# Closing multiplies and second norms on GpSimd, early second queries and a later column of ones, in two transformer layers on one core

## The chip, the cores and the metric

One Trainium2 chip, one of its cores. A core has TensorE (matmuls; PE in the profile, PEld for its weight loads), VectorE (DVE), ScalarE (ACT), GpSimd (POOL), SyncE (SP, which here only issues DMAs), an on-chip memory (SBUF) and an accumulator memory for matmuls (PSUM). The metric is the time of one execution in microseconds; less is better.

## What is computed

Two equal layers. Each is attention with a residual, then a token mixer with a residual. The input is 2048 tokens x 640; 32 heads of width 20; the hidden width of the mixer is 1536. Weights are the same in both layers.

```python
def _A_ref(x, wqkv, wo):                       # attention
    qkv = (x @ wqkv) ... q, k, v = qkv[0], qkv[1], qkv[2]
    scores = jnp.einsum("bhqd,bhkd->bhqk", q, k) * (Dh ** -0.5)
    o = jnp.einsum("bhqk,bhkd->bhqd", _softmax(scores), v)
    return o ... @ wo
def _B_ref(x, w1, b1, w2, b2):                 # mixer over tokens
    u = _gelu(jnp.einsum("bsd,sf->bdf", _layernorm(x), w1) + b1)
    return (jnp.einsum("bdf,fs->bds", u, w2) + b2) transposed
x = x + _A_ref(_layernorm(x), A_wqkv, A_wo)
x = x + _B_ref(_layernorm(x), B_w1, B_b1, B_w2, B_b2)      # and both once more
```

The mixer norms x before `_B_ref` and again inside it; the kernel does both norms in one pass, and this is what the text calls the second norm (`ln_proc` with `twice`).

## The kernel before, in words

**Work.** The scores of one head group (4 heads), one block of 512 queries and one tile of 128 keys are a *unit* of four *cells*, each 128 x 512. A layer has 4 x 8 x 16 = 512 units, 2048 cells. TensorE writes scores into tiles S of three or two cells in turn (`emit_S`, `s_matmul`, L703). ScalarE turns a tile into exponentials P (`emit_exp`, L773). Some cells go to VectorE instead (`ve_admit`, L547): their scores lie in the bank Dt, and VectorE and GpSimd work out 2^x by a polynomial, two cells (a pair) at a time: ew (L563), shift to ey (L661, on GpSimd, or on VectorE by L589), square (L593), et (L597), result Pd. For Pd, GpSimd may first write a half (L644, `ve_base`) to which VectorE adds (L614); otherwise VectorE forms it in one longer step (L616). TensorE multiplies P and Pd by the values with a column of ones (Vaug) into acc (L1326, `emit_PV`), so acc holds the products and the sum of the exponentials.

**Closing a run.** The 16 units of a head group and query block are a *run*. When a run closes, `finish_run` (L791) makes VectorE transpose acc (L810), add an earlier part of the run if there is one (L818), take reciprocals (L823), multiply (`scaled`, L826) and transpose into attnT (L834). The out-projection (L1117, in the last query block L1155 and L960) adds the residual. `ln_proc` (L880) then norms x: statistics (L886, L889), aggregate (L893), variance (L898 for the second norm, L901), the power -1/2 on GpSimd (L903), and the apply (L907) on VectorE. After that come the products with w1 (L1068), which `end_tiles` (L950) ends together with the last out-projection.

**Order.** All engines run in an order that the program works out while it is built. It keeps a clock for each engine (`pem`, `dvm`, `acm`, `port`) with a planned duration of each step. VectorE's work is a list of `Proc`s, each with a rank and steps; `pump` takes the ready one with the lowest rank. A step with a fourth element true is *locked*: it does not start before the planned end of GpSimd's job (`port["pool"]`). When a step of at least 0.45 us that isn't locked starts, `ve_shift` may give GpSimd one job beside it (a shift, or else a base); `after_vector` makes that job wait for the VectorE instruction before it. How many cells VectorE takes follows from its planned backlog. TensorE fills the time between scores with queued work (`add_fill`: projections, out-projection, mixer products), by priority, and with matmuls on zeros (L762) where little is queued.

**Feeds.** `TokenFeed` starts layer 0: loads and norms tokens, transposes them (L1225), projects keys and queries (L1177) and values (L1201). At its start ScalarE clears the pad columns of Vaug, and VectorE sets the column of ones (`zero_values`, L1546). `MixFeed` starts layer 1 from the mixer of layer 0 (L1753 to L1775, then `y_fill`, L1685). While tokens arrive, attention already runs on the first four head groups of query blocks 0 and 1 (`early_qbs`), as far as keys and queries are there. The queries of block 1 are queued in `t_fill` (L1249) with the priority `base[tb] + 16.0 + 8.0 * g - 4`; a lower number goes first.

**The ends of a layer.** After the last exponential the rest of the queue is emptied with three PSUM banks (`tail_alloc`, L1458), then `end_tiles` adds the last head group's out-projection and norms the last two token tiles.

Of the kernel before, what the change touches and what calls it, by code (L numbers as in the profile page):

```python
# [25 lines left out]
DH = 20  # L26
# [39 lines left out]
VE_SPARE = 6  # L66
VE_ADD = (1.22, 1.03, 0.69)
POOL_DMA = 0.9

HOLD = 3  # L70
WARM_WAVES = 14
# [10 lines left out]
def kernel(  # L82
# [141 lines left out]
    def attention(st, x_in_ap, x_mid, uacc_l, feed, feed_stack):  # L224
# [40 lines left out]
        acm = dict(t=feed.act_free, over=0.0, next=0.06, procs=[])  # L265
        port = dict(pool=0.0, t=0.0)
        pieces = deque()
        acc_free = [0.0]
        kready, vready = {}, {}
        work = deque()  # L270
# [389 lines left out]
        def shift(engine, out_ap, in_ap):  # L660
            return engine.tensor_scalar(out=out_ap, in0=in_ap, scalar1=MANT_K / FIX, scalar2=-MANT_K * MANT_S,  # L661
                                        op0=ALU.mult, op1=ALU.add)

        def ve_shift(at, self_cost):
# [126 lines left out]
        def finish_run(run):  # L791
# [24 lines left out]
            def added(end):  # L816
                dst = box["T1"] if whole else part_view((qb, g))
                nc.vector.tensor_tensor(out=cols(dst), in0=cols(box["T1"]), in1=cols(part_view((qb, g))), op=ALU.add)  # L818

            def recip(end):  # L820
                box["v"] = box["T1"].rearrange("p (c i) -> p c i", i=32)
                box["r"] = ntmp.tile([128, 16], F32, name="rden")
                nc.vector.reciprocal(out=box["r"][:, 0:nb], in_=box["v"][:, :, DH])  # L823

            def scaled(end):
                nc.vector.tensor_tensor(out=T2[:, 0:nb, 0:DH], in0=box["v"][:, :, 0:DH],  # L826
                                        in1=box["r"][:, 0:nb].unsqueeze(2).to_broadcast([128, nb, DH]), op=ALU.mult)

            def back(end):
                if c0 == 0:  # L830
# [21 lines left out]
            def turned(end):  # L852
                if rest:
                    p = Proc(norm_rank(run), rest, end + DVE_NEXT, after=after if whole else None,
                             allow=lambda me: not whole or (bool(late) and (len(me.steps) > 1 or at_live[0] < NG + 4)))
                    p.norm = True
                    submit(p)
            first.after = turned
            first.allow = lambda me: not any(p in dvm["procs"] for p in ahead)
# [20 lines left out]
        def ln_proc(src, twice, get_dst, rank, ready, after, allow_apply=None, on_act=False, cheap=0.0):  # L880
# [14 lines left out]
            def veps(e):  # L895
                v = stat.tile([128, 1], F32, name="veps")
                if twice:
                    nc.vector.tensor_scalar(out=v[:], in0=box["mv"][:, 1:2], scalar1=1.0 + LN_EPS,  # L898
                                            scalar2=LN_EPS * LN_EPS, op0=ALU.mult, op1=ALU.add)
                else:  # L900
                    nc.vector.tensor_scalar_add(out=v[:], in0=box["mv"][:, 1:2], scalar1=LN_EPS)  # L901
                box["r"] = stat.tile([128, 1], F32, name="rstd")
                nc.gpsimd.tensor_tensor(out=box["r"][:], in0=v[:], in1=mhalf[:], op=ALU.pow)  # L903
                port["t"] = max(port["t"], e + POOL_NEXT) + 0.55

            def apply(e):
                nc.vector.tensor_scalar(out=get_dst(), in0=src, scalar1=box["mv"][:, 0:1],  # L907
                                        scalar2=box["r"][:, 0:1], op0=ALU.subtract, op1=ALU.mult)

            def shift(e):  # L910
                box["n"] = stat.tile([128, 1], F32, name="nmr")
# [15 lines left out]
            submit(Proc(rank, steps, ready, after=last,  # L927
                        allow=allow_apply and (lambda me: len(me.steps) > 1 or on_act or allow_apply())))

        def do_ln2(tt, x1s, end):  # L930
            def dst():
# [285 lines left out]
        def t_fill(tt, h_bf, ready, done):  # L1217
# [235 lines left out]
        for t in sums:  # L1453
            zero_wave(t[:, 0:512], True, True)
            zero_wave(t[:, 512:D], True, True, HALF / 2, D - 512)
        tail_banks = [sums[0][:, 1024:1536], None, None]

        def tail_alloc():  # L1458
            bank = tail_banks.pop()
            return bank if bank is not None else Dbank.alloc() if len(tail_banks) == 1 else misc.alloc()  # L1460
# [10 lines left out]
    class TokenFeed:  # L1471
        groups = 4
        early_qbs = (0, 1)
        ve_early = True
        act_helps = True
        act_free = 0.0
        warm_until = 5.6
# [28 lines left out]
        def begin(self, cx):  # L1506
# [36 lines left out]
            def zero_values(e):  # L1543
                nc.scalar.memzero(Vv[:, :, :, DH:VW])
                nc.scalar.memzero(Vv[:, :, 4 * self.groups, 0:32 - VW])
                cx.submit(cx.Proc(2.6, [(0.49, lambda e: nc.vector.memset(Vv[:, :, :, DH:DH + 1], 1.0), 0.0)], e + 5.0))  # L1546
# [46 lines left out]
    class MixFeed:  # L1593
        groups = 4
        early_qbs = (0, 1)
        ve_early = False
        act_helps = True
        act_free = 0.0
        warm_until = 0.0
# [283 lines left out]
```

## Time and profile before

| | |
|---|---|
| median of 3 runs | 1754.15 us (1754.06 to 1754.17) |
| the profiled execution | 1754.05 us |
| its span | 1752.3 us |
| TensorE busy | 1677.7 us (96%) |
| ScalarE busy | 1665.0 us (95%) |
| VectorE busy | 1534.9 us (88%) |
| GpSimd busy | 592.0 us (34%) |
| granted TensorE clock | full, in every slice |
| chain of work that ended last | ScalarE 50%, TensorE 25%, issue 22% |

Busy time is the time in which an engine worked on an instruction; instructions of one engine overlap a little, so single durations add up to more. A row of the groups names line, engine, operation, result and inputs, count, busy time, mean of one in ns, and the engine's idle time just before with what ended it. A row of the stretches names from and to, length, and for each engine busy time and instructions, then granted clock, DMA share and GB/s. A row of the timeline names start, duration, engine, line and what it is, and in brackets the idle time before it.

### The profile page before, as it was taken

The numbers are of one execution on the slowest core, as the hardware profiler recorded it, in microseconds if no ns is written. First come the engines' busy times: TensorE is split into PE (matmuls) and PEld (weight loads), VectorE is DVE, ScalarE is ACT, GpSimd is POOL, SyncE is SP. The second block draws the span as 40 slices with busy tenths as digits, with TensorE's granted clock in tenths as the row PEclk, the third lists the DMA queues.
The fourth block names the chain that finished last, engine by engine and source line by source line (L and its number), as shares of the span: only waits on it lengthen the run. The fifth ranks groups of instructions, "written<-read, shape, count | busy, mean of one in ns | idle before, by whom it ended". The sixth has DMA issues, their size and how long they took to land.

```text
span 1752.3 us, 43289 instructions
## 1 busy us (share of the span) xinstructions
PE 1677.7 (96%) x17891; PEld 663.4 (38%) x17891; DVE 1534.9 (88%) x2491; ACT 1665.0 (95%) x1498; POOL 592.0 (34%) x936
## 2 busy tenths in 40 slices
PE   8999999999999999999999999999999999999999
PEld 3333333333333344444434433233333333444455
DVE  7789999999999999998543469999999999999973
ACT  8999999999999999999779999999999999999970
POOL 2243443353544343332000023434434443434310
PEclk9999999999999999999999999999999999999999
DMA  4020000000122010133322100001001220101445
GB/s 117 9 24 10 1 2 2 24 24 2 35 66 82 25 47 3 39 97 97 125 69 75 65 11 1 1 2 43 20 2 61 82 76 6 62 3 40 120 122 178
DMA packets 103014, 81.87 MB, mean 47 GB/s; under 512 B 50976, under 2 KB 87456, under 8 KB 102816
## 3 DMA queue, kind: packets, MB, share of 16 engines
q1 hardware_dynamic: 97280, 71.22, 13.5%
q0 software_dynamic: 5536, 7.88, 1.5%
q8 instruction: 140, 2.29, 0.5%
q14 instruction: 58, 0.48, 0.1%
HBM read 55.48 MB, written 23.59 MB: 45 GB/s over the span
## 4 chain that ended last, share of the span: by engine, by line
ACT 50%; PE 25%; issue 22%; DVE 2%; DMA 1%; POOL 0%; SPq 0%; ACTq 0%; DVEq 0%
ACT P L773 50%; PE S L703 7%; PE acc L1326 4%; PE misc L1068 2%; PE ya L1766 2%; PE misc L1177 2%; PE acc L762 2%; PE um L1753 1%; PE Dt L1177 1%; PE ya L1775 1%; PE yb L1766 1%; DMA w2s<-in_B_w_dram 1%; PE misc L1117 0%; PE misc L1685 0%; PE misc L1201 0%
## 5 line engine op out<-in xcount | busy, mean ns | idle before, releaser
L773 ACT ACTIVATE P<-S 128x1536 bf16<-128x1536 f32 (+1 forms) x1430 | 1617.4, 1369 | 13.5 <-PE S L703 13.0
L703 PE MATMUL S<-QTq,KT 32*128 32x512 bf16 (+1 forms) x4449 | 575.6, 337 | 60.9 <-ACT P L773 44.4
L661 POOL TENSOR_SCALAR ey<-ew 128x512 f16<-128x512 uint16 x516 | 320.6, 621 | 689.6 <-DVE et L597 306.4
L703 PEld LDWEIGHTS <-KT 32*128 32x128 bf16 x5127 | 229.6, 91 | 524.6 <-issue 497.0
L563 DVE TENSOR_SCALAR ew<-Dt 128x512 int32<-128x512 f32 x524 | 357.0, 681 | 22.3 <-PE Dt L703 14.8
L1326 PE MATMUL acc<-P,Vaug 128*32 128x512 bf16 (+1 forms) x4442 | 363.3, 343 | 0.3 <-DVE Vaug L370 0.3
L762 PE MATMUL acc<-zr,zw 128*32 128x512 bf16 x4256 | 328.1, 382 | 1.2 <-POOL zr L155 1.2
L597 DVE SCALAR_TENSOR_TENSOR et<-ey,ew 128x1024 int16<-128x1024 f16 x262 | 325.6, 1243 | 2.8
L644 POOL TENSOR_SCALAR Pd<-ew 128x512 int16<-128x512 int16 x317 | 196.8, 627 | 161.6 <-DVE et L597 42.4
L703 PE MATMUL Dt<-QTq,KT 32*128 32x512 bf16 (+1 forms) x678 | 201.4, 333 | 0.0
L593 DVE TENSOR_TENSOR ey<-ey 128x1024 f16<-128x1024 f16 x262 | 188.3, 719 | 1.4 <-POOL ey L661 0.3
L1326 PEld LDWEIGHTS <-Vaug 128*32 128x32 bf16 x5120 | 102.7, 94 | 175.4 <-issue 161.4
L762 PEld LDWEIGHTS <-zw 128*32 128x32 bf16 x4476 | 111.5, 96 | 97.9 <-issue 52.5
L616 DVE SCALAR_TENSOR_TENSOR Pd<-ew,et 128x1024 int16<-128x1024 int16 (+1 forms) x134 | 134.6, 1005 | 0.6
L614 DVE TENSOR_TENSOR Pd<-Pd,et 128x1024 int16<-128x1024 int16 (+1 forms) x189 | 121.8, 645 | 5.8 <-POOL Pd L644 3.8
L903 POOL TENSOR_TENSOR rstd<-veps,mhalf 128x1 f32<-128x1 f32 x60 | 49.4, 824 | 224.6 <-DVE veps L901 197.2
L1326 PE MATMUL acc<-Pd,Vaug 128*32 128x512 bf16 (+1 forms) x678 | 102.9, 336 | 1.4 <-DVE Pd L614 1.2
L1177 PE MATMUL misc<-hh,wq_pad 128*128 128x512 bf16 x290 | 84.0, 383 | 0.0
L1068 PEld LDWEIGHTS <-w1st 128*128 128x128 bf16 x672 | 52.9, 97 | 58.2 <-issue 45.3
L1177 PE MATMUL misc<-hh,wk_pad 128*128 128x512 bf16 x255 | 74.0, 383 | 0.0
L1068 PE MATMUL misc<-x1last,w1st 128*128 128x320 bf16 x384 | 73.0, 302 | 0.0
L1117 PE MATMUL misc<-wo_pad,attnT 128*128 128x320 bf16 x384 | 72.3, 302 | 0.2 <-DVE xin L1129 0.2
(145 smaller groups left out, 1180.4 us busy)
## 6 DMA issues: line engine op xcount, KB each, us to landing
w2s<-in_B_w_dram SPq DMA_DIRECT2D x16, 768.0 KB
uacc<-ustg POOLq DMA_DIRECT2D x24, 320.0 KB, 2.6
x1in<-xd SPq DMA_DIRECT2D x24, 320.0 KB
w1st<-in_B_w_dram SPq DMA_DIRECT2D x24, 256.0 KB
xd<-x2s SPq DMA_DIRECT2D x16, 320.0 KB
xin<-xd SPq DMA_DIRECT2D x16, 320.0 KB
w1st<-in_B_w_dram SPq DMA_DIRECT2D x24, 192.0 KB
xd<-x1s SPq DMA_DIRECT2D x12, 320.0 KB
```

The source lines that it names most:

```text
L563: nc.vector.tensor_scalar(out=w[:, slot, :], in0=Dt[:, :], scalar1=127.0 * FIX, scalar2=0.0, op0=ALU.add, op1=ALU.max)
L593: nc.vector.tensor_tensor(out=y, in0=y, in1=y, op=ALU.mult)
L597: nc.vector.scalar_tensor_tensor(out=box["t"][:, 0:512 * k], in0=ve_y.pop(p)[:, 0:512 * k], scalar=MANT_C * MANT_K ** 2, in1=frac, op0=ALU ...
L616: nc.vector.scalar_tensor_tensor(out=bits, in0=whole[:, lo:hi], scalar=128.0, in1=t, op0=ALU.mult, op1=ALU.add)
L644: after_vector(nc.gpsimd.tensor_scalar(out=bits, in0=whole, scalar1=128.0, scalar2=0.0, op0=ALU.mult, op1=ALU.add))
L661: return engine.tensor_scalar(out=out_ap, in0=in_ap, scalar1=MANT_K / FIX, scalar2=-MANT_K * MANT_S, op0=ALU.mult, op1=ALU.add)
L703: pe(nc.tensor.matmul(out_ap[:, c0:c0 + w], lhsT=KT[32 * j:32 * j + 32, g, kt * 128:(kt + 1) * 128], rhs=get_QT(st, qb)[32 * j:32 * j + 32 ...
L762: pe(nc.tensor.matmul(bank[32 * j:32 * j + 32, 0:w], lhsT=zw[:], rhs=zr[:, :, 0:64].to_broadcast([128, w // 64, 64]), start=start, stop=st ...
L773: nc.scalar.activation(out=P[:, 0:ncs, :].rearrange("p a b -> p (a b)"), in_=St[:, 0:ncs, :].rearrange("p a b -> p (a b)"), func=ACT.Exp, ...
L1068: pe(nc.tensor.matmul(t[:, 0:w], lhsT=w1_of[(p, ft)][:, sti, :], rhs=rows_in[sti][:, c0:c1], start=(sti == 0), stop=(sti == n_in - 1)))
L1177: pe(nc.tensor.matmul(t[:, :], lhsT=wpad[:, dt_, g, :], rhs=hT[:, dt_, tb * 512:(tb + 1) * 512], start=(dt_ == 0), stop=(dt_ == NDT - 1)))
L1326: pe(nc.tensor.matmul(acc[32 * j:32 * j + 32, a0:a0 + w], lhsT=Vaug[:, (kt * H + hh_) * VW:(kt * H + hh_) * VW + 32], rhs=P[:, slot, c0:c0 ...
```

## The change

Four edits.

1. A step may be offered to GpSimd as a job (`offer`). `ve_shift` looks for such a job first (`pool_job`); where one is taken, GpSimd runs the step, the `Proc` goes on without it, and the shift or base that might have stood there comes later or not at all. If GpSimd hasn't taken it 3 us after it is ready (`POOL_GRACE`), VectorE does it. Offered are the multiply of a closed run, except in the last three runs, and the apply of the second norm.
2. In layer 1, the queries of block 1 get a priority below all others (`early_q = -5.5`), so that they are projected as soon as their tokens are there. In layer 0 (`early_q = None`) the priority is the old one.
3. In layer 0, the column of ones is set 8 us instead of 5 us after the pads, by the planned clock.
4. `tail_alloc` goes round three banks, instead of handing out each once.

```diff
+POOL_APPLY = 0.75
+POOL_SCALED = 0.75
+POOL_GRACE = 3.0
...
+        def offer(proc, fn, cost, ready):
+            if not in_attention[0]:
+                return None
+            job = dict(fn=fn, cost=cost, ready=ready, proc=proc)
+            jobs.append(job)
+            proc.ready = ready + POOL_GRACE
+            return job
...
+        def pool_job(at):
+            if port["t"] > at + POOL_LATE:
+                return False
+            job = next((job for job in jobs if job["ready"] <= at + POOL_LATE), None)
+            if job is None:
+                return False
+            jobs.remove(job)
+            after_vector(job["fn"](nc.gpsimd))
+            done = max(at + POOL_NEXT, job["ready"], port["t"]) + job["cost"]
+            port["pool"] = port["t"] = done
+            proc = job["proc"]
+            proc.steps.popleft()
+            proc.ready = done + POOL_TO_DVE
...
         def ve_shift(at, self_cost):
+            if jobs and pool_job(at):
+                return
...
+            def scaled_on(engine):
+                return engine.tensor_tensor(out=T2[:, 0:nb, 0:DH], in0=box["v"][:, :, 0:DH],
+                                            in1=box["r"][:, 0:nb].unsqueeze(2).to_broadcast([128, nb, DH]), op=ALU.mult)
...
                 nc.vector.reciprocal(out=box["r"][:, 0:nb], in_=box["v"][:, :, DH])
+                if runs.index(run) < len(runs) - 3:
+                    box["job"] = offer(box["proc"], scaled_on, 0.15 + (POOL_SCALED - 0.15) * part, end + POOL_NEXT)
...
                 port["t"] = max(port["t"], e + POOL_NEXT) + 0.55
+                if twice:
+                    box["job"] = offer(box["proc"], apply_on, POOL_APPLY, e + POOL_RSTD)
...
-                            proj_fill("Q", g, tb, base[tb] + 16.0 + 8.0 * g - 4, at, fed=True)
+                            proj_fill("Q", g, tb, base[tb] + (8.0 * g + 12.0 if feed.early_q is None else 0.01 * g + feed.early_q),
+                                      at, fed=True)
...
-        tail_banks = [sums[0][:, 1024:1536], None, None]
+        tail_banks = [misc.alloc, Dbank.alloc, lambda: sums[0][:, 1024:1536]]
+        tail_used = [0]
...
-                cx.submit(cx.Proc(2.6, [(0.49, lambda e: nc.vector.memset(Vv[:, :, :, DH:DH + 1], 1.0), 0.0)], e + 5.0))
+                cx.submit(cx.Proc(2.6, [(0.49, lambda e: nc.vector.memset(Vv[:, :, :, DH:DH + 1], 1.0), 0.0)], e + 8.0))
```

More of the change, by code (lines that the diff above doesn't have):

```diff
@@ L267, in attention @@
         pieces = deque()
+        jobs = deque()
         acc_free = [0.0]
@@ L662, in shift, with taken @@
                                         op0=ALU.mult, op1=ALU.add)
+        def offer(proc, fn, cost, ready):
[5 more added lines that the diff above has]
+            return job
+        def taken(job):
+            if job is not None:
+                jobs.remove(job)
[5 more added lines that the diff above has]
+                return False
+            jobs.remove(job)
+            after_vector(job["fn"](nc.gpsimd))
[4 more added lines that the diff above has]
+            proc.ready = done + POOL_TO_DVE
+            if not proc.steps:
+                dvm["procs"].remove(proc)
+                if proc.after is not None:
+                    proc.after(done)
+            return True
         def ve_shift(at, self_cost):
+            if jobs and pool_job(at):
+                return
             if (not pieces or pieces[0][3] + POOL_NEXT > at + POOL_LATE or port["t"] > at + POOL_LATE or
@@ L823, in recip @@
                 nc.vector.reciprocal(out=box["r"][:, 0:nb], in_=box["v"][:, :, DH])
+                if runs.index(run) < len(runs) - 3:
+                    box["job"] = offer(box["proc"], scaled_on, 0.15 + (POOL_SCALED - 0.15) * part, end + POOL_NEXT)
             def scaled(end):
-                nc.vector.tensor_tensor(out=T2[:, 0:nb, 0:DH], in0=box["v"][:, :, 0:DH],
-                                        in1=box["r"][:, 0:nb].unsqueeze(2).to_broadcast([128, nb, DH]), op=ALU.mult)
+                taken(box.get("job"))
+                scaled_on(nc.vector)
             def back(end):
@@ L856, in turned @@
                     p.norm = True
+                    box["proc"] = p
                     submit(p)
@@ L904, in veps, with apply_on @@
                 port["t"] = max(port["t"], e + POOL_NEXT) + 0.55
+                if twice:
+                    box["job"] = offer(box["proc"], apply_on, POOL_APPLY, e + POOL_RSTD)
+            def apply_on(engine):
+                return engine.tensor_scalar(out=get_dst(), in0=src, scalar1=box["mv"][:, 0:1],
+                                            scalar2=box["r"][:, 0:1], op0=ALU.subtract, op1=ALU.mult)
             def apply(e):
-                nc.vector.tensor_scalar(out=get_dst(), in0=src, scalar1=box["mv"][:, 0:1],
-                                        scalar2=box["r"][:, 0:1], op0=ALU.subtract, op1=ALU.mult)
+                taken(box.get("job"))
+                apply_on(nc.vector)
             def shift(e):
@@ L926, in ln_proc @@
                 last = after
-            submit(Proc(rank, steps, ready, after=last,
-                        allow=allow_apply and (lambda me: len(me.steps) > 1 or on_act or allow_apply())))
+            box["proc"] = Proc(rank, steps, ready, after=last,
+                               allow=allow_apply and (lambda me: len(me.steps) > 1 or on_act or allow_apply()))
+            submit(box["proc"])
         def do_ln2(tt, x1s, end):
@@ L1455, in attention @@
             zero_wave(t[:, 512:D], True, True, HALF / 2, D - 512)
-        tail_banks = [sums[0][:, 1024:1536], None, None]
+        tail_banks = [misc.alloc, Dbank.alloc, lambda: sums[0][:, 1024:1536]]
+        tail_used = [0]
         def tail_alloc():
-            bank = tail_banks.pop()
-            return bank if bank is not None else Dbank.alloc() if len(tail_banks) == 1 else misc.alloc()
+            if tail_used[0] >= len(tail_banks) and len(held) > 1:
+                force(held.pop(1))
+            tail_used[0] += 1
+            return tail_banks[(tail_used[0] - 1) % len(tail_banks)]()
         room = pem["t"] + 1.3
@@ L1474 @@
         ve_early = True
+        early_q = None
         act_helps = True
@@ L1596 @@
         ve_early = False
+        early_q = -5.5
         act_helps = True
```

## The prediction, as it was made before the result

> **What bounds the kernel now.** I read the groups of instructions by shape first, then the busy time by stretch, then what ScalarE and VectorE waited for. By stretch (length, then busy us and instructions of TensorE, its weight loads, VectorE, ScalarE, GpSimd):
>
> ```profile
> 0.00:16.00 16.00, 12.63 (x133) 5.91 (x133) 11.42 (x38) 9.82 (x20) 5.48 (x17) 1.00 0.69 201
> 16.00:817.00 801.00, 768.32 (x8483) 291.78 (x8486) 757.22 (x1200) 800.26 (x707) 311.06 (x482) 1.00 0.12 32
> 817.00:853.00 36.00, 34.23 (x304) 19.44 (x296) 27.56 (x65) 23.15 (x30) 4.38 (x8) 1.00 0.59 194
> 853.00:901.00 48.00, 46.43 (x355) 20.18 (x354) 21.37 (x44) 36.99 (x34) 1.65 (x3) 1.00 0.23 75
> 901.00:1681.00 780.00, 749.62 (x8113) 288.83 (x8105) 685.60 (x1085) 779.72 (x690) 268.33 (x424) 1.00 0.12 38
> ```
>
> ScalarE is busy 800.26 of 801 and 779.72 of 780 us: in both long stretches the exponentials follow each other without a gap, and the span is their sum plus the places where ScalarE has none: the first 16 us, the change of layers, two holes in the feed of layer 1, and the last 71 us. VectorE is 95% busy in the first stretch, but it sets only how many of the 4096 cells (128x512 scores) it takes from ScalarE. So an edit is worth what it changes in ScalarE's exponentials, or at one of those edges.
>
> ```profile
> L773 ACT ACTIVATE P<-S 128x1536 bf16<-128x1536 f32 (+1 forms) x1430 | 1617.4, 1369 | 13.5 <-PE S L703 13.0
> ```
>
> 524 cells go to VectorE (L563 x524), 3572 to ScalarE. Singles overlap (mean 1369 ns each, but 1617.4 us busy for 1430), so I split the busy time: the 128x1536 form averages 1580 ns and the 128x1024 form 1160, about 0.42 us a cell; I use 0.427, which leaves (1617.4 - 3572 x 0.427) / 1430 = 0.065 us per instruction.
>
> **The multiplies and the second norm on GpSimd.** The order of the built programs tells what moves. VectorE loses 59 multiplies (L826, 128x320) and 28 applies (L907); 57 of GpSimd's own Pd steps (L644, 317 to 260) give up their places for them. VectorE then forms more results in one step instead of adding to a finished half: L616 at 128x1024 +32, L614 -28. VectorE: -59 x 0.552 - 28 x 0.70 + 32 x 1.275 - 28 x 0.739 = -32.6 - 19.6 + 40.8 - 20.7 = -32 us. It spends some of it: 6 more cells (6 x 0.681 + 3 x (1.243 + 0.719) = 10.0), and two more partial runs to transpose and add (2 x 1.25), 4 more shifts of its own (1.7): in all some -18 us of 1535. What matters is the 6 cells. ScalarE loses 4 cells and one instruction in layer 0, 2 cells and two instructions in layer 1: 6 x 0.427 + 3 x 0.065 = **-2.76 us**, all on the path.
>
> GpSimd's price is in no row. The nearest are its one-input ops and VectorE's multiply:
>
> ```profile
> L661 POOL TENSOR_SCALAR ey<-ew 128x512 f16<-128x512 uint16 x516 | 320.6, 621 | 689.6 <-DVE et L597 306.4 <-DVE ey L593 138.4 <-DVE Pd L616 119.2
> ...
> L826 DVE TENSOR_TENSOR T<-T,rden 128x320 bf16<-128x320 f32 x62 | 34.2, 552 | 0.1
> ```
>
> A norm is one input of 640: 0.621 x 640/512 = 0.78 us. A multiply of 320 is at least 0.621 x 320/512 = 0.39 (inputs for nothing) and at most three such passes, 1.16. I take two passes, 0.78, since it has two inputs. GpSimd gains 59 x 0.78 + 28 x 0.78 - 57 x 0.627 = +32 us on 592: free of its own work. Each job stands behind a VectorE step of 0.45 us or more that reads PSUM or transposes; VectorE's locked steps wait until the planned end of it. Behind it on VectorE stands the transpose to attnT (L834), for which the planner does other steps first. Cover: VectorE's 43.8 us of idle time in the first stretch. I cost it at nothing; without the cover it is the slower rival below.
>
> [...]
>
> ```profile
> 1677.55 1.53 DVE L597 SCALAR_TENSOR_TENSOR et<-ey,ew 128x1024 int16<-128x1024 f16 x1
> ```
> ```profile
> 1677.39 0.62 POOL L644 TENSOR_SCALAR Pd<-ew 128x512 int16<-128x512 int16 x1 [2.39 <-DVE ey L593]
> ```
> ```profile
> 806.76 1.23 DVE L597 SCALAR_TENSOR_TENSOR et<-ey,ew 128x1024 int16<-128x1024 f16 x1
> ```
>
> Beside GpSimd the same step took 1.53 instead of 1.23 us: a collision costs some 0.3 us of VectorE, 87 of them 26 us, less than its idle time.
>
> **Layer 1's second queries first.** ScalarE's holes in the feed:
>
> ```profile
> 883.44 7.37 ACT L773 ACTIVATE P<-S 128x1024 bf16<-128x1024 f32 x7 [8.34 <-PE S L703]
> 892.16 7.38 ACT L773 ACTIVATE P<-S 128x1536 bf16<-128x1536 f32 x7 [1.35 <-PE S L703]
> 900.59 2.37 ACT L773 ACTIVATE P<-S 128x1024 bf16<-128x1024 f32 x2 [1.05 <-PE S L703]
> ```
>
> TensorE's order in the feed is the same in both programs up to 889.5 us, so the 8.34 us stay: the tokens that the second queries need are transposed only at 883 to 887 us. Then, where a key projection and a value projection stood (10 matmuls, 4 more for the run that ends), two query projections stand (9 matmuls). The score matmul waits for the copy of the first: projection at 889.48, its end about 890.7, copy 0.69, score at about 891.5 instead of 891.67: -0.17. With second queries ready, four times as many units are open; before, two score tiles stood side by side in the order at 900 us (the mark of a refill after a hole), after they don't until all tokens are in: the 1.05 us go. What is late next is the keys of block 1, pushed back by 20 projection matmuls (4.3 us); the open units cover 16 x 1.8 us. **-1.2 us**; between 0 and -1.3.
>
> **The column of ones later.** VectorE's one long wait in the head:
>
> ```profile
> 8.01 0.15 DVE L901 TENSOR_SCALAR veps<-mv 128x1 f32<-128x1 f32 x1
> 10.06 0.48 DVE L1546 MEMSET Vaug<- 128x512 bf16 x1 [1.90 <-ACT hh L366]
> 10.14 0.55 DVE L907 TENSOR_SCALAR h_bf<-x0in,mv,rstd 128x640 bf16<-128x640 bf16 x1
> ```
>
> The fourth norm stands behind the memset, though its rstd is there at 8.79. If the 1.90 us are the memset's own, that norm runs at 8.9, its transposes at 10.2 (behind fixed zero waves) instead of 10.75, the hh copy at 10.7 instead of 11.24, the key projection at 11.4. The order also puts the copy to KT ahead of the sixth norm, which waited for GpSimd: KT at 12.9 instead of 14.03, QTq at 13.95 instead of 14.63, first score 14.86 instead of 15.54: -0.68. If the wait stays with the place, the norm waits as the memset did, and QTq slips by some 0.2: +0.2. If the memset waits 1.9 us again at its new place: +0.7. The row names the memset; I take **-0.6**.
>
> **What the new order does to layer 0's tail.** More late products remain: behind the last values matmul and ahead of the last out-projection (L960) stand 7 product matmuls (L1068), where none stood; both groups use the same bank, and VectorE empties the first only after the attnT transpose (end 818.85). Layer 1 of before shows this very sequence: the add at 1683.35, products from 1683.85, L960 at 1684.66, statistics at 1685.48, 4.08 us after the last exponential. In layer 0 of before, statistics start at 819.45, 2.63 us after the end at 816.82. So layer 0 pays 4.08 - 2.63 = **+1.5 us**; down to 0 if the add slips ahead of the transposes. Layer 1's tail has one group more, but the same wait: its third group waits for the same add, so 0. The bank list now cycles: its first three picks are the old ones, and no more are used: 0.
>
> **Sum.** -2.76 - 1.2 - 0.6 + 1.5 = -3.06 us on the profiled execution's 1754.05 (span 1752.3, 1.75 around it): 1751.0. The median of the runs is 0.1 above it: forecast **1751.1 us**. About 0.2%, 3.5 us, is what a measurement of this kernel can tell from no change: faster is below 1750.6, slower above 1757.7.
>
> **Rivals.**
> A, the tail wait hides and the head gains in full: -2.76 - 1.2 - 0.7 + 0 = -4.7, 1749.5 us. For it: ScalarE's table load and copies stand beside the tail. Against: layer 1 shows the wait. Chance 0.24.
> B, the edges give nothing: the memset waits again (+0.7), the hole at 900 us moves instead of closing: -2.76 + 0.7 + 1.5 - 0.2 = -0.8, 1753.4 us. For it: the wait's cause isn't plain in the trace. Chance 0.18.
> C, slower: GpSimd's jobs hold VectorE. Place: the locked step behind each of the 44 jobs of a layer. Price: the job's time over the planned 0.75. VectorE's idle time from 100 to 800 us is 700 - 679.6 = 20.4 us, with 9 us of relief about 29 per layer, so it decides from 29 / 44 = 0.67 us over plan, a job of 1.42 us. At four passes (1.55 us) it is 44 x 0.8 - 29 = 6 per layer: +12 - 3 = +9, 1763 us. Against: three passes are 1.16. Chance 0.08.
> That the change does not do what it says is out: the order shows the 87 moved instructions.
>
> **How the numbers follow.** Forecast 0.50, A 0.24, B 0.18, C 0.08. The range takes in A and B whole and leaves C out: 1749.2 to 1753.8. Faster by over 0.2%: A and a fifth of the forecast's own cases, 0.34; slower: C, 0.08; within: 0.58.
>
> **What would show it.** Right: 1427 exponentials; no hole of ScalarE near 900 us, the one of 8.3 us still there; first exponential near 15.3 us; statistics of L980 some 4.1 us after layer 0's last exponential; GpSimd multiplies of 0.4 to 1.2 us; ScalarE over 99.9% busy in both long stretches. Wrong: exponentials waiting for scores in the middle of a stretch, with VectorE's L614 or L616 in TensorE's waits; GpSimd multiplies over 1.4 us; a memset that waits again.

## The result: slower by 0.95%

The changed kernel takes **1770.97 us** (median of 5 runs, 1769.35 to 1772.53) against 1754.15 before; the ratio is 1.0095, with a 95% interval of 1.0084 to 1.0106. The forecast was 1751.1. The profiled execution is the fastest of the five, 1769.35 us with a span of 1767.6.

Where the 15.3 us of its span come from is read off three kinds of moments: the first and the last exponential of each layer, and the end. The columns of kernels further down are those of the experiments; "holes" are ScalarE's idle times of over 0.1 us between two exponentials of the layer.

| us | before | after | step of the prediction | measured |
|---|---|---|---|---|
| start to first exponential | 15.97 | 17.60 | -0.6 | **+1.63** |
| layer 0's exponentials (holes) | 800.84 (0.44) | 808.70 (8.70) | -1.77 | **+7.86** |
| layer 0's last to layer 1's first | 36.45 | 37.96 | +1.5 | +1.51 |
| layer 1's exponentials (holes) | 828.13 (10.99) | 832.21 (14.73) | -0.98 - 1.2 | **+4.08** |
| layer 1's last to the end | 70.88 | 71.08 | 0 | +0.20 |

The same table by stretch, for the changed kernel, cut at the same events:

```profile
0.00:18.00 18.00, 14.05 (x135) 6.51 (x136) 12.26 (x39) 10.21 (x20) 5.48 (x17) 1.00 0.57 172
18.00:826.00 808.00, 766.87 (x8365) 288.01 (x8363) 761.87 (x1166) 798.98 (x706) 363.00 (x502) 1.00 0.12 32
826.00:864.00 38.00, 35.64 (x321) 20.37 (x320) 28.44 (x67) 23.46 (x31) 4.38 (x8) 1.00 0.56 187
864.00:912.00 48.00, 46.40 (x344) 19.61 (x339) 21.30 (x43) 38.19 (x35) 1.64 (x3) 1.00 0.23 75
912.00:1696.00 784.00, 750.86 (x8165) 289.64 (x8158) 686.79 (x1051) 778.63 (x688) 312.37 (x436) 1.00 0.13 38
```

ScalarE, without a gap in the long stretches before, is now idle for 9 us of the first and 5 of the second, and GpSimd (the last busy column) has grown by 52 and 44 us instead of the 16 that were costed for each. The groups of GpSimd's instructions say which of its new work is dear:

```profile
L858 POOL TENSOR_TENSOR T<-T,rden 128x320 bf16<-128x320 f32 x59 | 43.5, 737 | 89.1 <-DVE et L601 59.8 <-DVE ey L597 15.0 <-DVE Pd L620 11.9
L953 POOL TENSOR_SCALAR x1last<-x1s,mv,rstd 128x640 bf16<-128x640 f32 x8 | 23.2, 2902 | 3.7 <-DVE et L601 3.0
L953 POOL TENSOR_SCALAR x1last<-xin,mv,rstd 128x640 bf16<-128x640 f32 x8 | 21.9, 2742 | 2.0 <-issue 1.0 <-POOL rstd L947 0.4
```

The multiply takes 0.737 us, as costed (0.78). The second norm takes 2.5 us where nothing disturbs it and **2.77 on average** (77.5 us for 28), where 0.78 was costed and 0.75 is what the planner believes. One of them, in order of time:

```profile
365.74 2.50 POOL L953 TENSOR_SCALAR x1last<-x1s,mv,rstd 128x640 bf16<-128x640 f32 x1
368.33 1.31 POOL L665 TENSOR_SCALAR ey<-ew 128x512 f16<-128x512 uint16 x2
369.72 1.20 POOL L648 TENSOR_SCALAR Pd<-ew 128x512 int16<-128x512 int16 x2
370.95 0.69 DVE L618 TENSOR_TENSOR Pd<-Pd,et 128x1024 int16<-128x1024 int16 x1 [2.65 <-POOL Pd L648]
371.70 0.39 PE L1378 MATMUL acc<-Pd,Vaug 128*32 128x512 bf16 x2 [2.61 <-DVE Pd L618]
372.73 2.54 ACT L810 ACTIVATE P<-S 128x1536 bf16<-128x1536 f32 x2 [2.57 <-PE Dt L740]
```

Read it downwards: the norm holds GpSimd until 368.2; four integer steps that were planned some 2 us earlier follow it; VectorE's add waits 2.65 us for them; TensorE's next matmul reads the result of that add and waits 2.61; and the score matmuls stand behind that matmul in TensorE's order, so ScalarE waits 2.57. The norm is off the path itself; what stood in its queue was not.

### The profile page after: what moved, and what is told of

Its sections match the earlier page's. It is cut to its first block, busy times and chain, and to the rows that moved or that the text cites. A ratio compares the mean times of both kernels' runs of the same rounds, so it can differ in the third digit from the quotient of the medians.

```text
span 1767.6 us, 43164 instructions
## 1 busy us (share of the span) xinstructions
PE 1681.1 (95%) x17865; PEld 661.8 (37%) x17865; DVE 1542.7 (87%) x2426; ACT 1664.6 (94%) x1495; POOL 688.0 (39%) x968
## 4 chain that ended last, share of the span: by engine, by line
ACT 46%; PE 22%; issue 21%; DVE 8%; POOL 3%; DMA 0%; ACTq 0%; POOLq 0%; DVEq 0%
ACT P L810 46%; PE S L740 6%; PE acc L1378 3%; PE ya L1823 2%; PE acc L799 2%; DVE et L601 2%; PE misc L1119 2%; PE misc L1228 1%; DVE ew L567 1%; POOL ey L665 1%; POOL x1last L953 1%; DVE ey L597 1%; DVE Pd L618 1%; PE um L1810 1%; DVE Pd L620 1%
## 5 line engine op out<-in xcount | busy, mean ns | idle before, releaser
L810 ACT ACTIVATE P<-S 128x1536 bf16<-128x1536 f32 (+1 forms) x1427 | 1617.0, 1363 | 28.1 <-PE S L740 22.4
L665 POOL TENSOR_SCALAR ey<-ew 128x512 f16<-128x512 uint16 x518 | 331.0, 639 | 555.7 <-DVE et L601 253.5
L740 PEld LDWEIGHTS <-KT 32*128 32x128 bf16 x5133 | 226.0, 91 | 529.7 <-issue 505.6
L567 DVE TENSOR_SCALAR ew<-Dt 128x512 int32<-128x512 f32 x530 | 360.8, 681 | 20.4 <-PE Dt L740 15.3
L601 DVE SCALAR_TENSOR_TENSOR et<-ey,ew 128x1024 int16<-128x1024 f16 x265 | 335.5, 1266 | 3.5
L648 POOL TENSOR_SCALAR Pd<-ew 128x512 int16<-128x512 int16 x260 | 161.6, 626 | 113.1 <-DVE ey L597 37.3
L597 DVE TENSOR_TENSOR ey<-ey 128x1024 f16<-128x1024 f16 x265 | 192.7, 727 | 2.8 <-POOL ey L665 2.5
L620 DVE SCALAR_TENSOR_TENSOR Pd<-ew,et 128x1024 int16<-128x1024 int16 (+1 forms) x165 | 177.7, 1077 | 0.3
L618 DVE TENSOR_TENSOR Pd<-Pd,et 128x1024 int16<-128x1024 int16 (+1 forms) x160 | 105.8, 662 | 19.2 <-POOL Pd L648 16.8
L1228 PE MATMUL misc<-hh,wk_pad 128*128 128x512 bf16 x275 | 79.5, 383 | 0.0
L858 POOL TENSOR_TENSOR T<-T,rden 128x320 bf16<-128x320 f32 x59 | 43.5, 737 | 89.1 <-DVE et L601 59.8
```

The costliest lines, as they stand in the source:

```text
L567: nc.vector.tensor_scalar(out=w[:, slot, :], in0=Dt[:, :], scalar1=127.0 * FIX, scalar2=0.0, op0=ALU.add, op1=ALU.max)
L597: nc.vector.tensor_tensor(out=y, in0=y, in1=y, op=ALU.mult)
L601: nc.vector.scalar_tensor_tensor(out=box["t"][:, 0:512 * k], in0=ve_y.pop(p)[:, 0:512 * k], scalar=MANT_C * MANT_K ** 2, in1=frac, op0=ALU ...
L618: nc.vector.tensor_tensor(out=bits, in0=bits, in1=t, op=ALU.add)
L620: nc.vector.scalar_tensor_tensor(out=bits, in0=whole[:, lo:hi], scalar=128.0, in1=t, op0=ALU.mult, op1=ALU.add)
L648: after_vector(nc.gpsimd.tensor_scalar(out=bits, in0=whole, scalar1=128.0, scalar2=0.0, op0=ALU.mult, op1=ALU.add))
```

## The experiments

Every time is a median, with its ratio to the kernel before and the 95% interval; segments (first exponential, layers, holes, stretches between) are those of the table above and come from the profiled execution. The edits of experiments 6 and 8 leave VectorE, ScalarE and GpSimd with the instructions of the changed kernel in the same order (but for the small step that experiment 6 adds on GpSimd). In the others the program plans a new order, so what they compare are two orders.

**1. The norms back on VectorE** (no_norm).

```
             def veps(e):
                 ...
-                if twice:
-                    box["job"] = offer(box["proc"], apply_on, POOL_APPLY, e + POOL_RSTD)
```

> The changed kernel with its 28 second norms back on VectorE; GpSimd keeps the 59 multiplies. Theory N (the norm's price): a norm on GpSimd takes 2.5 us alone in the trace of the changed kernel, planned at 0.75, and the integer steps queued behind it make VectorE and TensorE wait. Then the holes in ScalarE's exponentials fall from 8.7 to about 0.4 us in layer 0 and from 14.7 to about 9.7 in layer 1, no stretch of half clock is left in the middle, and the time falls by 8.3 + 5.0 = 13 us to about 1757.5. Rival L (every job on GpSimd locks VectorE out, multiplies too): 59 of the 87 jobs are still there, so at least half of the loss stays, 1763 or more.

Measured: 1752.95 us, 0.9991 (0.9983 to 1.0000); holes 1.23 and 9.82 us, layers 799.95 and 825.98. With all 59 multiplies still on GpSimd the loss is gone: theory N, and rival L falls. It gave back 18 us rather than 13. In the profiled executions the layers give 15.0, of which 12.4 are holes. A hole costs more than itself, since the exponential behind it no longer overlaps the one ahead (in the changed kernel they average 1363 ns, and 1427 of them are busy 1617.0 us: some 0.23 us of overlap each, an estimate from these): without their holes, layer 0 takes 808.70 - 8.70 = 800.00 in the changed kernel and 798.72 here, layer 1 817.48 and 816.16. The two tails give 2.1 more (36.81 and 70.10), where the new order leaves fewer products. The head takes 2.3 back: this execution has its first exponential at 19.88, behind a stretch of half clock (see the last section).

**2. The multiplies back on VectorE, the norms left on GpSimd** (no_mul; the offer in `recip` removed).

> The changed kernel with its 59 multiplies back on VectorE; GpSimd keeps the 28 second norms. Theory N (the norm's price): nothing is mended, 1768 to 1773 us, with two to four holes of over 1 us behind a norm. Rival L (the multiplies hold VectorE): two thirds of the jobs are gone and the time falls below 1764.

Measured: 1763.26 us, 1.0052 (1.0038 to 1.0066); holes 5.48 and 11.95. Theory N missed by 5 us, and the bound set for rival L was met by 0.7; but the rival's reason is out, since experiment 1 has the same 59 multiplies and loses nothing. With the norms on GpSimd and the multiplies off it the kernel is 10 us above experiment 1, where it is the other way round, and 7 above experiment 11, which has neither there (and its ones in words). The multiplies, harmless by themselves, cost 8 more beside norms. That fits two kinds of work standing in one line, but the orders differ too; how the 8 us come about in detail stays open.

**3. The memset back at its old time** (mem_back).

```
-                cx.submit(cx.Proc(2.6, [(0.49, lambda e: nc.vector.memset(Vv[:, :, :, DH:DH + 1], 1.0), 0.0)], e + 8.0))
+                cx.submit(cx.Proc(2.6, [(0.49, lambda e: nc.vector.memset(Vv[:, :, :, DH:DH + 1], 1.0), 0.0)], e + 5.0))
```

> The changed kernel with only the memset of the column of ones back at its old time (e + 5.0). Theory M: the 1.9 us of idle time ahead of the memset belong to the memset, wherever it stands (1.90 us before, 1.87 us in the changed kernel); at its new place they delay the values' copy, which holds the bank that the query projection needs. Then the wait stands ahead of the fourth norm again and the first exponential is back at about 16.0 us from 17.6: the time falls by about 1.6 us, to 1769. Rival: the first exponential comes late for the order of the other copies; it stays at 17 us or later and the time does not move.

Measured: 1768.19 us, 1.0078 (1.0066 to 1.0091); first exponential at 16.00. Theory M: the wait ahead of the memset is 1.88 us here, 1.87 in the changed kernel, wherever it stands. The time fell by 2.8 us rather than 1.6, because the new order also shortens the stretch behind layer 0, from 37.96 to 36.73.

**4 and 5. Single forms of instruction** (forms, forms2), each repeated in a kernel that computes nothing else.

> No part of the computation: the kernel writes zeros and runs single forms of instruction six times each, on GpSimd alone, on VectorE alone, then both together. Theory 1 for the norm's 2.5 us: operands that are a column in memory instead of a constant make it slow; then the same 640 elements with constants take about 0.78 us (0.621 x 640/512), all forms with columns 2.5 us, at 320 elements 1.3. Theory 2: 32-bit input makes it slow; then the constants don't help, and the bf16 input does. Theory 3: subtract then multiply is slow; then multiply then add is fast. The memset of every 24th bf16 element: if the 1.9 us belong to its store pattern, each of the six shows them, or takes about 2.4 us, and the one in 32-bit words or in a row doesn't; if they belong to the first of its kind, one of six does; if to its place in the head, none does. [...]

> No part of the computation: zeros are written, and single forms run six times each. GpSimd, 640 fp32 elements to bf16, one after the other: if only the pair multiply-add has a fast way, all other pairs take 2.49 us and single operations somewhere between; if subtraction is the slow one, all pairs without it take 0.87. VectorE's memset of every 24th 16-bit element: if the wait ahead of it is its own store, it grows with the elements: 0.47 us at 128, 0.94 at 256, 1.87 at 512; if it is a fixed cost, 1.87 each; at every second element the same as at every 24th if single 16-bit elements cause it. Beside a stream of two-input adds on VectorE: the fast form stays below 1.3 us, the slow one at 2.5 to 3.0 us, as in the changed kernel (2.77).

GpSimd's groups of the first run (640 fp32 elements to bf16; the shapes are in the lines):

```profile
L73 POOL TENSOR_SCALAR g<-srcb,mv,rstd 128x640 bf16<-128x640 bf16 x6 | 16.5, 2750 | 0.0
L79 POOL TENSOR_TENSOR g<-src,other 128x640 bf16<-128x640 f32 x6 | 9.1, 1524 | 0.0
L77 POOL TENSOR_SCALAR g<-src,mv,rstd 128x320 bf16<-128x320 f32 x6 | 8.6, 1429 | 0.0
L75 POOL TENSOR_SCALAR g<-src,rstd,mv 128x640 bf16<-128x640 f32 x6 | 5.2, 871 | 0.0
```

L73 and L77 are subtract then multiply, from bf16 and on 320 elements; L75 is multiply then add, on operands in memory like the norm's. Undisturbed, subtract then multiply took 2.49 us with columns, 2.34 with constants (L69), 2.49 from bf16: theories 1 and 2 fall, and theory 3 holds. The second run, by pairs, undisturbed:

| GpSimd, 640 elements | us |
|---|---|
| multiply then add, with constants | 0.72 |
| add then multiply; multiply then multiply | 0.87; 0.87 |
| one operation alone: multiply, add or subtract | 1.88 |
| subtract then multiply; multiply then subtract; subtract then add | 2.50; 2.50; 2.50 |

Of these, a pair with a subtraction is the slow one (2.50 us against 0.72 to 0.87), and a single operation (1.88) is slower than a fast pair. Beside a plain stream of two-input adds on VectorE, in the second run, the fast pair took 1.50 to 1.57 us (below 1.3 was expected), the slow one 3.06 to 3.21; VectorE's adds took 0.82 to 1.39. So GpSimd's instructions lengthened by 0.6 to 0.7 us there. No add ran beside an idle GpSimd, so VectorE's part of the price is not shown.

VectorE's memsets in the second run alternate with such adds, which take 0.8 to 1.0 us of each pair (up to 1.2 at 128 elements). A pair with a memset of every 24th 16-bit element takes 1.25 to 1.42 us at 128 elements, 1.84 at 256 and 3.01 at 512; with every second element 1.42 at 512; with 32-bit words at the same 512 places 1.55 (first run). So the slow one grows with its elements and costs 2.0 us or more at 512, where the word costs some 0.75 and the narrow stride 0.5. The memset's row says 0.485 in all the forms of 512: the rest of a slow one shows as idle time ahead of it.

**6. The norm as multiply then add on GpSimd** (norm_madd).

```
+            def apply_gp(engine):
+                n = stat.tile([128, 1], F32, name="nmr")
+                after_vector(engine.tensor_scalar(out=n[:], in0=box["mv"][:, 0:1], scalar1=box["r"][:, 0:1],
+                                                  scalar2=-1.0, op0=ALU.mult, op1=ALU.mult))
+                return engine.tensor_scalar(out=get_dst(), in0=src, scalar1=box["r"][:, 0:1],
+                                            scalar2=n[:, 0:1], op0=ALU.mult, op1=ALU.add)
```

> The changed kernel with its 28 second norms still on GpSimd, but written as multiply then add (x * rstd + n, with n = -mean * rstd from a 128x1 step of GpSimd ahead of it). In the run of single forms multiply then add took 0.87 us for 640 elements where subtract then multiply took 2.49. Theory N' (the loss is the norm's duration beyond its plan of 0.75): norm and small step together take some 1.0 to 1.2 us, the holes behind norms go, and the time comes near the one with the norms on VectorE (1752.95): 1753 to 1756. [...]

```profile
L954 POOL TENSOR_SCALAR nmr<-mv,rstd 128x1 f32<-128x1 f32 x28 | 15.3, 547 | 10.4 <-DVE et L601 7.3 <-DVE ey L597 0.4 <-DVE Pd L620 0.4
L956 POOL TENSOR_SCALAR x1last<-x1s,rstd,nmr 128x640 bf16<-128x640 f32 x8 | 9.8, 1220 | 0.8
```

Measured: 1756.70 us, 1.0013 (1.0004 to 1.0022); holes 1.12 and 9.96, layers 800.46 and 827.24. The norms are as many and in the same places in the queue; at 1.14 + 0.55 us instead of 2.77 they cost nothing that shows as a hole. Theory N': a norm on GpSimd does not cost by its place in the queue alone, and as nothing but the form of the norm has changed, this is the plainest proof of the cause. The time is 0.7 above the expected range. Of the 2.6 us between the profiled spans of this kernel and experiment 1, 1.8 lie in the layers and 2.1 in the tails, whose order is still the changed kernel's (37.96 and 71.08); the head, with half clock in both executions, is 1.3 shorter here (18.61).

**7. The planner told the price** (plan28: `POOL_APPLY = 2.8`).

> The changed kernel with the planned price of a norm on GpSimd set to 2.8 us, what it takes; the order is planned anew: 27 norms and 57 multiplies still go to GpSimd, ScalarE gets 1432 exponentials with 3576 cells (5 and 12 more than the change: 12 x 0.427 + 5 x 0.065 = 5.4 us). Theory S (the loss was the surprise: steps planned behind a norm that came 2 us late): holes of over 0.5 us go, 1757 to 1761, the 5.4 us above the kernel without norms on GpSimd. Rival W (the load itself: GpSimd has no 28 x 2.8 us to give): holes remain and the time stays above 1764.

Measured: 1762.55 us, 1.0047 (1.0034 to 1.0060), between the two. Layer 0 is as S says (holes 1.12, 802.35 with two more instructions); layer 1 keeps holes of 13.06, one of 1.98 among them, and its 832.65 us are no less than the changed kernel's. Of the changed kernel's 18.0 us over experiment 1, 8.4 come back. Of the 9.6 that remain, the 12 cells that VectorE gives up are 5.4 by the estimate above, and 4.2 are left for the load. By that reckoning most of the loss was the surprise; no run separates the two.

**8. The first bank of the tail changed** (tail_d).

```
-        tail_banks = [misc.alloc, Dbank.alloc, lambda: sums[0][:, 1024:1536]]
+        tail_banks = [Dbank.alloc, misc.alloc, lambda: sums[0][:, 1024:1536]]
```

> The changed kernel, with only the order of the tail's banks changed: the first late product group takes the bank of VectorE's cells, not the one whose last sum VectorE has yet to empty. Theory: layer 0's statistics start 4.15 us after the last exponential because the products wait 1.24 us for VectorE's add; then they start some 1.2 us earlier, the stretch from the last exponential of layer 0 to the first of layer 1 falls from 38.0 to 36.7 us, the last one from 71.1 to 70; the time falls by 1.2 to 2.4 us from 1771. Rival: the products themselves (7 matmuls) are the delay, and it stays within 0.5 us.

Measured: 1770.14 us, 1.0091 (1.0077 to 1.0105). In layer 0 the statistics start 2.79 us after the last exponential instead of 4.15, and the stretch takes 36.58 us: the wait for the bank is the cause there. In layer 1, with one group more, they start at 5.09 instead of 4.28, and its tail takes 71.89. The median is 0.8 us below the changed kernel's, whose runs lie 3.2 apart: the forecast of 1.2 to 2.4 is not shown.

**9. Norms on VectorE, the ones in 32-bit words at the old time** (no_norm_word).

```
+            Vw = Vaug[:, 0:NKT * H * VW].bitcast(mybir.dt.uint32).rearrange("p (k h c) -> p k h c", k=NKT, h=H)
...
+                cx.submit(cx.Proc(2.6, [(0.9, lambda e: nc.vector.memset(Vw[:, :, :, DH // 2:DH // 2 + 1], 16256), 0.0)], e + 5.0))
```

The planned cost of the memset is 0.9 us here; in experiments 10 and 11 it is 0.49, as before.

> The changed kernel with its second norms on VectorE (1752.95 in the run before), and the column of ones written at its old time in words of 32 bits (the one and the zero beside it) instead of every 24th 16-bit element. In the run of single forms each 16-bit memset waited 1.87 us, each 32-bit one 0.42. Theory M (the wait belongs to the store of single 16-bit elements): 0.4 us ahead of the memset in place of 1.9, the fourth norm runs some 1.5 us earlier, the first exponential comes at 15.3 to 15.6 us against 16.0 before and 17.2 to 19.9 with the memset late; time 1749 to 1751. Rival (the wait is the place): 1.9 us again, first exponential at 16.0, 1751.

Measured: 1752.61 us, 0.9992 (0.9983 to 1.0001). The wait is 0.41 us and the fourth norm runs at 8.93 instead of 10.14, but the first exponential comes at 15.92, as in the kernel before: what is late next is the token tile that lands at 10.5 and the values' copy at 12.45, which frees the query projection's bank. The wait was the memset's, and removing it there brought the first exponential no closer. The time is 1752.61, not the 1749 to 1751 of theory M.

**10 and 11. The same words at the new, late time** (no_norm_word8), **and without the multiplies on GpSimd** (no_jobs_word8).

> The changed kernel with its second norms on VectorE, and the column of ones written at its new, late time, but in words of 32 bits; the order of all other instructions is that of the run with the norms back (1752.95, first exponential at 19.9 us, behind 1.87 us of wait and a stretch of half clock at 15.6 us). Theory: of the late memset's delay 1.4 us go, TensorE's wait for the values' copy falls from 2.5 to about 1 us, no stretch of half clock follows, and the first exponential comes at 16.1 us: span about 1749, time 1750 to 1751, the sum of the prediction without GpSimd's norms. Rival: the half clock or another copy keeps the first exponential at 17.5 us or later, and the time stays at 1752 to 1753.

> As the kernel beside it (norms on VectorE, ones in 32-bit words at the late time), and the 59 multiplies back on VectorE too: nothing of this change is left on GpSimd. ScalarE has one exponential more, 2 cells and one instruction of ScalarE, 0.9 us. Theory: the multiplies on GpSimd are worth just that, 0.5 to 1.5 us: this kernel is slower than the one beside it by that. Rival L' (the multiplies cost VectorE more in waits than the cells return): this one is faster or within 0.3 us.

no_norm_word8: **1750.78 us, 0.9981 (0.9973 to 0.9990)**, faster than both kernels; first exponential at 15.88, layers 800.07 and 825.98, tails 36.45 and 70.10. It lies 0.3 from the forecast of 1751.1 us, but only layer 1 came out by the forecast's terms, so that nearness is luck: against the kernel before, the head gives 0.1 (0.6 forecast), layer 0 0.8 (1.8), its tail pays nothing (1.5), layer 1 gives 2.2 (2.2) and the last tail 0.8 (0). ScalarE waits for scores as little as before (13.0 us there):

```profile
ACT P L810 <- PE S L740: 13.4, 5, 8.3
```

no_jobs_word8: 1756.18 us, 1.0009 (1.0001 to 1.0018). The kernel with the multiplies on GpSimd is 5.4 us faster, not 0.9: the theory's figure and rival L' both fall. Of the 4.6 between the two profiled spans 1.4 lie in layer 0 and 3.5 in the last tail (73.61), whose statistics start 6.84 us after the last exponential, against 3.31: this order leaves 24 product matmuls for the tail, that of experiment 10 leaves 10. So most of the 5.4 us is the order, not the multiplies as such: experiment 2, also with the multiplies on VectorE, leaves 7 and its last tail takes 71.07.

**12. The early queries alone, on the kernel before** (before_early; with the cycling list of banks that they need).

> The kernel before with only layer 1's second queries first, and the list of the tail's banks that this needs. ScalarE has 1428 exponentials with 3569 cells (2 and 1 fewer: -0.6 us). Theory E: the holes of 1.35 and 1.05 us in the feed become one of 1.2, as in every run of the changed kernel so far: -1.2; the tail of layer 0 may pay up to 1.5 us for the late products. Together -1.8 to 0: 1752.3 to 1754.2. Rival: the hole moves and the queries give nothing, 1753.5 to 1755.5.

Measured: 1755.08 us, 1.0006 (0.9997 to 1.0015). This is the rival's range, but not for its reason. The hole at 900 us is gone; the one at 891 is 2.03 us, behind a stretch of half clock from 887.2; and the last tail takes 73.61: 24 product matmuls are left for it, as in experiment 11, where the kernel before leaves 10. In the profile the step gives 0.6 in layer 1 and loses 2.7 behind it. But that execution (1756.22) is one of three of the eleven at 1756.2 to 1756.3 us; the other eight, at full clock, take 1754.9 to 1755.1. So without the half clock the step gives some 1.7 in layer 1, an estimate from this difference of 1.2, and the tail's 2.7 outweigh it.

## Why the prediction was wrong

- **The step that failed** is the price "A norm is one input of 640: 0.621 x 640/512 = 0.78 us". It took GpSimd's constants-only multiply-add as the price of any one-input operation; the norm is a subtraction and a multiplication and takes 2.50 us, 2.77 on average. No row of the trace before shows such a pair on GpSimd (VectorE does it in 0.6 to 0.7), and its upper end was not kept as the text did for the multiply, at three passes. One-input operations on GpSimd took 0.72 to 2.50 us for the same 640 elements in experiments 4 and 5, so size and number of inputs did not give the price.
- **Rival C had the mechanism, not the job.** It let a long job hold VectorE's locked steps, but only for the multiply, and set the point from which it decides by a sum: 29 us of slack a layer. By that sum 14 norms at 2.0 us over plan (28 us) would still have hidden. They didn't: a norm is a delay of 2 us in a queue in order, the norms come in bunches (8 of layer 0's 14 between 347 and 493 us), and three times VectorE's add behind them met it in full. It waited 2.65, 3.68 and 3.22 us; TensorE's next matmul then waited 2.61, 2.83 and 1.87 (the second of these is an out-projection, which waits for the VectorE step behind that add), and ScalarE 2.57, 3.36 and 2.25. The first case is shown above; VectorE's rows of the other two:

```profile
657.54 0.69 DVE L618 TENSOR_TENSOR Pd<-Pd,et 128x1024 int16<-128x1024 int16 x1 [3.68 <-POOL Pd L648]
1235.34 0.42 DVE L618 TENSOR_TENSOR Pd<-Pd,et 128x512 int16<-128x512 int16 x1 [3.22 <-POOL Pd L648]
```

  Slack elsewhere in the layer doesn't help a wait here.
- **The head** was priced at both ends by the wait, +0.7 where "the memset waits 1.9 us again"; it did (1.87 us), and cost +1.63. The first half came out as written: norm at 8.84 (8.9), copy to hh at 10.60 (10.7), key projection at 11.35 (11.4). The error is what stood behind the memset at its new place, the values' copy, whose bank the query projection needs:

```profile
14.20 0.48 DVE L1602 MEMSET Vaug<- 128x512 bf16 x1 [1.87 <-ACT wq_pad L1615]
14.30 0.70 DVE L374 CAST Vaug<-misc 128x320 bf16<-128x320 f32 x1
...
16.43 0.68 DVE L376 TENSOR_SCALAR QTq<-misc 128x512 bf16<-128x512 f32 x1
```

- **The early queries** were right in their place: the hole of 8.34 us stays, the second is 1.2 (1.18 forecast), the third is gone, -1.2 in sum.

```profile
894.44 7.37 ACT L810 ACTIVATE P<-S 128x1024 bf16<-128x1024 f32 x7 [8.34 <-PE S L740]
903.02 3.71 ACT L810 ACTIVATE P<-S 128x1536 bf16<-128x1536 f32 x3 [1.21 <-PE S L740]
```

  Alone they also leave products to the last tail (73.61 us in experiment 12), a cost that the prediction did not name and that the whole change does not show (71.08).
- **Layer 0's tail** was right to 0.1 us: statistics 4.15 us after the last exponential (4.08 forecast), for the reason given; the first line is VectorE's add that frees the bank, the second its add of the products that TensorE could start only then, the third the statistics.

```profile
828.32 0.45 DVE L1127 TENSOR_TENSOR KT<-misc,KT 128x320 f32<-128x320 f32 x1
829.84 0.49 DVE L1127 TENSOR_TENSOR KT<-misc,KT 128x320 f32<-128x320 f32 x1 [1.07 <-PE misc L1119]
830.45 0.90 DVE L1031 BATCH_NORM_STATS2 bnst<-S 128x6 f32<-128x320 f32 x2
```

  The price belongs to this order: with the norms on VectorE (experiments 1 and 10) three products stand there instead of seven, and the stretch takes 36.81 and 36.45 us.

- **The cells** were right: without the holes' effect ScalarE's exponentials are busy 1614.8 us in experiment 1 against 1617.4, -2.6 for a forecast of -2.76. But the count says nothing of what moved them: 528 cells go to VectorE with nothing on GpSimd (experiment 11), 530 with the multiplies there, 524 before. So 4 of the 6 come from the rest of the order, not from the multiplies.

## What to carry to other kernels

Price an operation on another engine by a row with the same operations, not only the same size and number of inputs; where there is none, measure the form alone before anything is planned on it (0.87 and 2.50 us here for two pairs of operations on the same 640 elements). A shared queue in order can pass on a late job in full, however much idle time its stage has on average (three of 28 jobs did so here); ask what is queued behind the longest job, not only how much slack there is. When a stalled instruction is moved, its stall may go with it, as the memset's did (1.90 us of wait before, 1.87 at the new place), and the price is set by what stands behind it at the new place.

## What the hardware showed that was not expected

- GpSimd's pairs of operations on the same 640 elements took 0.72 to 0.87 us without a subtraction and 2.34 to 2.50 with one (experiments 4 and 5), and the norm could be turned into the fast kind (1.14 us and a small step of 0.55 in experiment 6, for 2.77).
- A memset of 512 single 16-bit elements 48 bytes apart cost some 2.0 to 2.4 us of VectorE, of which the row shows 0.485; at 4 bytes apart 0.5. By their rows, 512 elements of 16 or of 32 bits both take 0.485 us; the wait ahead is 1.87 us for the one and 0.42 for the other (experiment 4). Why wide strides of single elements are slow is open.
- Behind three waits of TensorE in the changed kernel (2.61, 2.83 and 1.87 us) the granted clock was 0.50 for 3.41 us. The lines are stretches of 3.41 us, the first column behind the length being TensorE's busy time, 1.00 or 0.50 the clock:

```profile
365.27:368.68 3.41, 3.28 (x25) 1.18 (x27) 3.04 (x7) 3.41 (x4) 3.22 (x3) 1.00 0.44 144
368.68:372.09 3.41, 0.80 (x12) 0.16 (x6) 1.14 (x2) 1.48 (x2) 2.44 (x5) 1.00 0.00 0
372.09:375.50 3.41, 3.41 (x17) 0.59 (x15) 3.38 (x6) 2.47 (x2) 2.31 (x3) 0.50 0.00 0
655.40:658.81 3.41, 0.58 (x9) 0.33 (x6) 1.27 (x3) 2.27 (x3) 2.44 (x5) 1.00 0.00 0
658.81:662.22 3.41, 3.41 (x24) 1.16 (x26) 3.41 (x8) 1.19 (x1) 2.24 (x3) 0.50 0.45 144
1232.25:1235.66 3.41, 1.60 (x15) 0.70 (x14) 0.32 (x1) 3.18 (x3) 3.06 (x2) 1.00 0.07 29
1235.66:1239.07 3.41, 3.25 (x10) 0.74 (x9) 3.41 (x8) 1.02 (x1) 1.55 (x3) 0.50 0.55 191
```

  The three stretches of half clock start 84 and 169 times 3.413 us apart: they fall on a grid of 3.41 us. Of the 517 stretches of that grid in this trace, the three with the least work of TensorE, 0.58, 0.80 and 1.60 us, were followed by half clock; the others have 1.92 us or more and were not. In the other traces, one of 1.71 us (experiment 7, from 1230.1) was followed by it and one of 1.77 (experiment 3, from 380.6) was not; two with more were, one of 2.55 in experiment 12, which stays unexplained, and one of 2.63 in experiment 7, itself at half clock. So a wait of some 2 us can cost twice, by where it falls. In the head TensorE waits 2.5 us for the values' copy in experiment 1 and in the changed kernel alike. In experiment 1's profile that left 1.47 us of work in the stretch up to 15.62, the clock was 0.50 in the one behind it, and the first exponential came at 19.88; in the changed kernel's the stretches there have 2.21 and 1.92 us of work and full clock, and it came at 17.60. Such stretches would account for the changed kernel's runs spreading over 3.2 us, where those of the kernel before lie within 1.2: the five have a mean granted clock of 0.997 to 0.995, and the longer ones the lower. That the spread has no other cause was not tried.
